# The second layer of an MLP by seven block products, with its weight factors streamed from DRAM and its output turned on VectorE

## The chip, the cores and the metric

The kernel runs on one core of a Trainium2 chip. The metric is device time in microseconds (us). A value is the median of the runs of one kernel; each run of the chip job also ran the kernel before beside it, on the same chip. "Span" is the length of a profiled execution, one to two microseconds shorter than its time.

Names: PE is TensorE's matmul side, PEld its weight loading, DVE VectorE, ACT ScalarE, POOL GpSimd, SP SyncE, which issues nearly all transfers from one in-order queue.

## The reference, cut to what matters

```python
# attention: batch 8, 12 heads, 448 tokens, head_dim 64; q and k RMS-normed, softmax(q k^T / 8) v
x = attn_out.transpose(0, 2, 1, 3).reshape(3584, 768)   # 8 images of 448 tokens
h = x @ w_in             # 768 x 2048
g = h - np.tanh(h)
out = (g @ w_out)        # 2048 x 768, float32
```

The weights arrive as float64 and are rounded to float32 on the chip.

## The kernel before

Image b's MLP runs in the gaps of image b+1's attention; a step is a pair of heads, six steps to an image. A generator yields after every matmul, and each step runs it for four gaps. Image 7's MLP has no attention beside it.

Layer one is already done by seven block products of eight: the matrices are cut in 2x2 blocks, sums and differences of blocks (the factors) are multiplied, and seven products do the work of eight. Image 0 rounds and combines the weight factors, stores them to DRAM, and every image loads them from there through a ring of SBUF tiles (cut):

```python
ring = pool("ring", bufs=8)
ORDER = (1, 6, 5, 2, 7, 3, 4)

def keep_weights():                 # called from weight(), some pieces after set j was combined
    j = kept[1]
    for p in ORDER:                 # seven stores of 384 KB in a row
        nc.sync.dma_start(out=w_in_dram[j, p], in_=built(j, p).rearrange("p f n -> p (f n)"))
    kept[1] = j + 1

def ring_load(to):
    for n in range(len(ring_tiles), min(to, len(ring_steps))):
        b, j, p = ring_steps[n]
        t = ring_tiles[ring_steps[n]] = ring.tile([P, 2, HC, P], F32, name="w_f")
        nc.sync.dma_start(out=t.rearrange("p f c n -> p (f c n)"), in_=w_in_dram[j, p])

def product(j, p, bank, first):     # inside hidden(b), layer one
    k = SETS * 7 * b + 7 * j + ORDER.index(p)
    if b == 0:
        weight(EARLY + k + 1)       # one more weight piece is rounded
    ring_load(k + 7)                # this product and the six after it
    w = ring_tiles[b, j, p]
    for f in range(2):
        for c in range(HC):
            nc.tensor.matmul(bank[:, f * HS : (f + 1) * HS], lhsT=w[:, f, c, :], rhs=moving[p](c), ...)
            ...
```

Layer two is plain. A 128-token tile of g is stationary, half a row of w_out (384 columns, resident in SBUF) moves, and the 64 left-over tokens of two images share a tile, so that images alternate between three and four tiles:

```python
def project(b):
    g = late["g"]
    ring_load(SETS * 7 * (b + 1) + 7)      # the next image's first factors
    units = [(t, n) for t in range(FULL + b % 2) for n in range(2)]
    ...
    for t, n in units:
        for f in range(CF):
            nc.tensor.matmul(ops[:, :HALF], lhsT=lhs[:, f, :], rhs=w_out_sb[f][:, d], ...)
        # ScalarE or VectorE copies the bank to o_sb, SyncE stores it in 1536 B rows
```

## Time and profile before

| | |
|---|---|
| time | 1610.07 us (1609.01 to 1610.49) |
| image 0's MLP beside image 1's attention | 119.6 to 336.7 us of the span |
| images 1 to 6 | 336.7 to 1456.6 us |
| image 7 alone, with the end | 1456.6 to 1608.6 us |
| TensorE / VectorE / GpSimd busy | 96% / 43% / 34% |

The prediction below shows the engine table, the slices and the windows. The first fence is from the page: the DMA row of the 40 slices (tenths of the 16 engines' time) and the queue that carries everything (packets, MB, share of 16 engines).

```profile
DMA  7664974135310452125411244015411144104200
...
q1 hardware_dynamic: 129472, 168.33, 34.6%
```

The row stands at four to nine tenths in slices 1 to 6 and mostly lower after. The second is from the view of the factor loads' source line up to the end of layer one of image 0 (100 to 228 us): who waited for these loads (us, times), and how long they took from issue to landing.

```profile
  POOL w_out L90: 3.8, 2
  PE mc L427: 2.8, 1
...
DMA to landing us min/median/max: 3.7/5.3/8.9
```

TensorE waited for a factor once, 2.8 us, although a load took up to 8.9 us here. Six products of lead, at least 13.6 us at 2.27 us each, covered the rest.

### The profile page before, as it was taken

How to read it: one execution, taken by the hardware profiler on the slowest of the kernel's cores; microseconds unless marked ns; L12 is line 12 of the kernel's file. 1: busy time of each engine (PE TensorE's matmuls, PEld its weight loads, DVE VectorE, ACT ScalarE, POOL GpSimd, SP SyncE). 2: the span in 40 equal slices, each digit the busy share in tenths (PEclk: the TensorE clock that was granted, in tenths of full speed). 3: DMA queues.
4: the chain of work that ended last, by engine and by line, in shares of the span. 5: the costliest groups of instructions: out<-in, count | busy, mean ns of one | idle time of the engine just before them, and what ended most of it. 6: DMA issues, size and time to landing. Idle time of an engine off the chain costs nothing.

```text
span 1608.6 us, 17479 instructions
## 1 busy us (share of the span) xinstructions
PE 1542.8 (96%) x6664; PEld 1018.9 (63%) x6664; DVE 697.1 (43%) x825; ACT 436.4 (27%) x829; POOL 549.8 (34%) x438
## 2 busy tenths in 40 slices
PE   3968799999999999999999999999999999999998
PEld 1327664478655776558855687558755578559954
DVE  6898888543432334234432343333433244221100
ACT  4553354223212232213311133123222123201100
POOL 6655665533422234223322233322432233211200
PEclk9999899999999999999999999999999999999999
DMA  7664974135310452125411244015411144104200
GB/s 197 184 222 148 339 248 125 54 106 154 100 32 28 119 149 91 44 63 153 127 50 32 67 140 148 28 43 151 140 57 32 41 144 145 45 10 142 74 20 22
DMA packets 129889, 169.54 MB, mean 105 GB/s; under 512 B 52485, under 2 KB 93445, under 8 KB 129797
## 3 DMA queue, kind: packets, MB, share of 16 engines
q1 hardware_dynamic: 129472, 168.33, 34.6%
q8 instruction: 55, 0.90, 0.2%
q14 instruction: 38, 0.30, 0.1%
q10 hardware_dynamic: 324, 0.00, 0.0%
HBM read 146.28 MB, written 22.02 MB: 105 GB/s over the span
## 4 chain that ended last, share of the span: by engine, by line
PE 82%; DVE 11%; issue 2%; DMA 2%; POOL 1%; ACT 1%; SPq 0%; ACTq 0%; DVEq 0%; POOLq 0%
PE mb L515 34%; PE mb L427 12%; PE ma L427 8%; PE mc L427 8%; PE sc L327 8%; PE sc L353 7%; DVE w_out L79 3%; PE sc L365 2%; DVE rd L370 2%; DVE w_out L78 1%; POOL sq L280 1%; DVE w_out L82 1%; DVE rr L281 1%; PE sc L303 1%; PE sc L307 1%
## 5 line engine op out<-in xcount | busy, mean ns | idle before, releaser
L515 PE MATMUL mb<-w_out,gT 128*128 128x384 f32 x1536 | 518.2, 492 | 0.0
L515 PEld LDWEIGHTS mb<-w_out,gT 128*128 128x128 f32 x1536 | 287.4, 191 | 221.5 <-issue 37.8
L332 ACT ACTIVATE p<-sc,rr 112x448 f32<-112x448 f32 x384 | 212.6, 636 | 380.4 <-PE sc L327 287.2
L327 PE MATMUL sc<-qT,kT 64*112 64x448 f32 x768 | 179.0, 575 | 5.0 <-DVE rd L370 4.3
L427 PE MATMUL ma<-xT,w_f 128*128 128x224 f32 x768 | 164.7, 362 | 16.9 <-DVE xT L376 11.1
L427 PEld LDWEIGHTS ma<-xT,w_f 128*128 128x128 f32 x768 | 146.4, 194 | 33.0 <-issue 13.7
L427 PE MATMUL mb<-tt,w_f 128*128 128x224 f32 x768 | 156.7, 357 | 5.3 <-DVE u L467 5.3
L370 DVE RECIPROCAL rd<-sc 128x448 f32<-128x448 f32 x42 | 124.0, 2953 | 86.7 <-PE sc L365 86.7
L284 POOL TENSOR_TENSOR rr<-rr,neg_half 112x16 f32<-112x16 f32 x48 | 140.0, 2916 | 50.2 <-DVE rr L283 47.0
L427 PEld LDWEIGHTS mb<-tt,w_f 128*128 128x128 f32 x768 | 144.9, 192 | 16.0 <-issue 8.6
L346 DVE TENSOR_TENSOR sum<-sum,p 112x896 f32<-112x896 f32 x84 | 99.8, 1188 | 111.5 <-ACT p L332 106.2
L280 POOL TENSOR_TENSOR sq<-k_nat 112x512 f32<-112x512 f32 x48 | 53.1, 1106 | 243.8 <-DMA k_nat<-in_k_dram 243.8
L353 PE MATMUL sc<-p,v_nat 112*64 112x448 f32 x672 | 133.4, 539 | 0.0
L327 PEld LDWEIGHTS sc<-qT,kT 64*112 64x112 f32 x768 | 65.1, 177 | 91.3 <-issue 68.7
L281 DVE TENSOR_REDUCE rr<-sq 112x8 f32<-112x512 f32 x96 | 65.6, 684 | 121.9 <-POOL sq L280 121.9
L468 POOL TENSOR_TENSOR u<-u,s 128x448 f32<-128x448 f32 x32 | 38.7, 1208 | 225.0 <-DVE u L467 219.7
L416 POOL TENSOR_TENSOR gT<-s,th 128x448 f32<-128x448 f32 x64 | 74.7, 1170 | 87.8 <-ACT th L414 87.8
L525 DVE COPY o_sb<-mb 128x384 f32<-128x384 f32 x28 | 15.6, 556 | 201.9 <-PE mb L515 201.9
L280 POOL TENSOR_TENSOR sq<-q_nat 112x512 f32<-112x512 f32 x48 | 49.9, 1040 | 142.6 <-DVE rr L281 142.6
L353 PEld LDWEIGHTS sc<-p,v_nat 112*64 112x64 f32 x672 | 48.3, 137 | 78.0 <-issue 76.8
L427 PE MATMUL mb<-xT,w_f 128*128 128x224 f32 x384 | 83.0, 360 | 2.5 <-DVE s L455 2.5
L515 PE MATMUL mb<-w_out,g_rest 128*128 128x384 f32 x256 | 85.4, 489 | 0.0
(79 smaller groups left out, 1493.2 us busy)
## 6 DMA issues: line engine op xcount, KB each, us to landing
w_f<-w_in SPq DMA_DIRECT2D x224, 384.0 KB, 3.3
w_raw<-in_moe_w_out_dram SPq DMA_DIRECT2D x32, 384.0 KB, 3.7
k_nat<-in_k_dram SPq DMA_DIRECT2D x96, 112.0 KB, 3.2
q_nat<-in_q_dram SPq DMA_DIRECT2D x48, 224.0 KB, 3.5
v_nat<-in_v_dram SPq DMA_DIRECT2D x48, 224.0 KB, 4.0
w_in<-w_out SPq DMA_DIRECT2D x28, 384.0 KB, 6.0
out_dram<-o_sb SPq DMA_DIRECT2D x48, 192.0 KB, 1.9
gT<-in_moe_w_in_dram SPq DMA_DIRECT2D x20, 384.0 KB, 5.8
```

Of the source, the lines that this page charges most:

```text
L79: nc.vector.tensor_scalar(out=bits, in0=bits, scalar1=4, scalar2=1, op0=ALU.logical_shift_left, op1=ALU.logical_shift_right)
L280: nc.gpsimd.tensor_tensor(out=sq, in0=rows, in1=rows, op=ALU.mult)
L281: nc.vector.reduce_sum(rr[:, i], sq, axis=AX.X)
L284: nc.gpsimd.tensor_tensor(out=rr2, in0=rr2, in1=neg_half, op=ALU.pow)
L327: nc.tensor.matmul(sc[:CP, :S], lhsT=kT[r, c * CP : (c + 1) * CP], rhs=qT[r, :], start=True, stop=True)
L332: nc.scalar.activation(p[:, h, i, :], tiles[h][:CP, :S], AF.Exp, scale=rr[:, 0, 2 * c + h : 2 * c + h + 1])
L346: nc.vector.tensor_tensor(out=t, in0=t, in1=part, op=ALU.add)
L353: nc.tensor.matmul(av[h * D : (h + 1) * D, :S], lhsT=v_nat[:, h, c, :], rhs=p[:, h, c % 2, :], start=(c == 0), stop=(c == NCH - 1),)
L370: nc.vector.reciprocal(rd, dn[:, :S])
L416: eng.tensor_tensor(out=g[:, f : f + 2, cols], in0=h, in1=th, op=ALU.subtract)
L427: nc.tensor.matmul(bank[:, f * HS : (f + 1) * HS], lhsT=w[:, f, c, :], rhs=moving[p](c), start=(first and f == 0 and c == 0), stop=(f == 1 ...
L515: nc.tensor.matmul(ops[:, :HALF], lhsT=lhs[:, f, :], rhs=w_out_sb[f][:, d], start=(f == 0), stop=(f == CF - 1),)
```

## The change

The intent: layer two also by seven products of eight, on blocks of half the features by half the tokens, in images 1 to 7. The weight factors, now the stationary side, are built once in image 0 and streamed from DRAM like layer one's; g and its combinations move, 224 columns at a time. The output then comes out as features by tokens; VectorE turns it in 32x32 squares, and four transfers per 128 features write rows of 32 floats. Image 0 keeps a plain layer two, turned as well (448 columns moving).

Smaller things go with it. The ring has six slots instead of eight, of larger tiles. The order of products is 1, 5, 6, 2, 7, 3, 4. In image 0 factors are loaded three products ahead instead of six, the sums of attention's steps 6 and 7 go to TensorE, and each half of image 0's MLP gets three steps of attention instead of two and four. A few edits to the first steps and to pools are left out. Cut to its core:

```diff
-    ring = pool("ring", bufs=8)
+    ring = pool("ring", bufs=6)
-    ORDER = (1, 6, 5, 2, 7, 3, 4)
+    ORDER = (1, 5, 6, 2, 7, 3, 4)
+    def combine_w_out(f):                      # image 0, second half of layer two; two ring tiles each
+        t = [ring.tile([P, 8 * P], F32, name="w_f") for _ in range(2)]
+        ...                                    # three VectorE and one GpSimd operation of 128x384
+        for n, count, src in (...):            # four stores in 512 B pieces
+            nc.sync.dma_start(out=w_out_dram[:, n : n + count, :, f, :]..., in_=src...)
+    def ring_load(key, ahead):
+        for n in range(len(ring_tiles), min(ring_steps.index(key) + ahead, len(ring_steps))):
+            ...
+            else:
+                nc.sync.dma_start(out=t, in_=w_out_dram[:, BLOCKS[p], j].rearrange("p f d -> p (f d)"))
     def add(s):
-        if s < NP:
+        if s < NP + 2:                         # sums of steps 6 and 7 go to TensorE
             sums[s] = []
+        def product(j, p, bank, first):        # now shared by both layers
+            if b == 0:
+                weight(EARLY + 7 * j + ORDER.index(p) + 1)
+            ring_load((b, layer, j, p), 4 if b == 0 else 5)
+            ...
+    def store(b, n, y):
+        nc.vector.transpose(out=o, in_=y)
+        for i in range(P // BL):               # four transfers of 128 B rows
+            nc.sync.dma_start(out=out[...].rearrange("(j t) d -> t j d", t=BL), in_=o[...])
     def gap_ns(s):
-        if b == 0:
-            return H_NS / 8 if s % NP < 2 else O_NS * FULL / (4 * (NP - 2))
+        if s < 2 * NP:                         # image 0: three steps for each layer
+            return H_NS / 12 if s % NP < 3 else 4 * S / ENGINE_NS * CD * CF / 12
     ...
```

## The prediction

> **What bounds the kernel now.** I read, in this order: the engine table and the slices of the page, then the windows view (busy time by engine over chosen stretches), the waits of TensorE in the long middle stretch, the chain that ended last, and the groups by shape. The profiled span is 1608.6 us, the timed median 1610.07 us.
>
> Engine table and slices:
>
> ```profile
> PE 1542.8 (96%) x6664; PEld 1018.9 (63%) x6664; DVE 697.1 (43%) x825; ACT 436.4 (27%) x829; POOL 549.8 (34%) x438
> ...
> PE   3968799999999999999999999999999999999998
> ...
> DVE  6898888543432334234432343333433244221100
> ```
>
> One slice is 40.2 us. TensorE is full from the sixth slice on. In slices 1 to 6 VectorE is at eight or nine tenths and TensorE has holes. So there are two regimes, and the border must be found. The windows view does that (columns: window, length, then busy us of each engine, granted clock, DMA share, GB/s):
>
> ```profile
> 119.00:228.00 109.00, 91.95 (x426) 76.85 (x427) 96.81 (x134) 45.75 (x95) 65.28 (x50) 0.90 0.74 245
> 228.00:336.80 108.80, 103.99 (x369) 51.32 (x367) 74.08 (x93) 39.06 (x77) 56.84 (x47) 0.95 0.36 106
> 336.80:1456.00 1119.20, 1119.20 (x4904) 745.23 (x4904) 415.83 (x449) 276.19 (x512) 335.91 (x272) 1.00 0.29 87
> 1456.00:1608.60 152.60, 146.72 (x594) 112.20 (x592) 15.28 (x25) 15.27 (x28) 18.93 (x17) 1.00 0.22 67
> ```
>
> The four stretches are: first layer of image 0, second layer of image 0, images 1 to 6 beside the attention of images 2 to 7, and image 7 alone. In the third, TensorE is busy for all 1119.20 us and VectorE for 37%. The waits view of TensorE's matmul side has no row at all there; its weight-load side waits almost only for "issue", which is load time beside running matmuls and not lost:
>
> ```profile
> PEld sc L353 <- issue: 66.2, 285, 0.2
> ...
> PEld sc L327 <- DVE s L455: 1.2, 6, 0.2
> ```
>
> So from 337 us on the time is TensorE's work and nothing else. The chain and the groups give what that work costs (line 427 is layer one by seven block products, 515 is the plain layer two):
>
> ```profile
> 1504.27 4.54 PE mb L427 x24
> ...
> 1520.16 82.57 PE mb L515 x256
> ```
> ```profile
> L515 PE MATMUL mb<-w_out,gT 128*128 128x384 f32 x1536 | 518.2, 492 | 0.0
> L427 PE MATMUL ma<-xT,w_f 128*128 128x224 f32 x768 | 164.7, 362 | 16.9 <-DVE xT L376 11.1
> ```
>
> Each f32 matmul of the program is two records. The group means of 362 and 492 ns overlap their neighbours; the pitch comes from the chain: 4.54/24 = 0.189 us for 224 columns, 82.57/256 = 0.3225 us for 384. Both are 0.84 ns per column. There is no fixed cost per matmul at either width, so columns can be counted.
>
> **What the Trainium skill says.** "TensorE: Matmul & The Clock Gate", section "Step-by-step: what each phase is for", says that the load of the next stationary tile runs beside the current matmul. The trace agrees at just the width that the new layer two will have: 24 records in 4.54 us, although their weight loads average 192 ns in the group list. "SBUF — State Buffer", section "SBUF: two separate sides", says that a VectorE operation with two SBUF inputs (or in a two-port mode) and a GpSimd operation reading SBUF lock each other out. The early trace agrees: the same VectorE operation of line 79 takes 0.36 us or 1.06 us there. "VectorE: DVE Perf Modes", section "The three transpose paths", gives 311 ns for a 128x128 bf16 turn by 32x32 blocks; no turn on VectorE is in this trace. "DMA: Bandwidth & Descriptors", section "Specifications", puts line rate at 512 B and more, with a read-modify-write below. The new output rows are 128 B; this trace has none of those (its stores are 1536 B rows), so their cost is open.
>
> **The change, part by part.**
>
> *Layer two, TensorE.* Before, image b takes 3 or 4 row tiles, on average 3.5 x 2 halves x 16 = 112 matmuls of 384 columns: 112 x 0.645 = 72.2 us. After, images 1 to 7 take 7 products x 3 sets x 8 = 168 matmuls of 224 columns: 168 x 0.378 = 63.6 us. Image 0 stays plain but turned, 96 matmuls of 448 columns: by 0.84 ns per column 0.752 us each, 72.2 us. So 7 x 8.6 = 60.3 us of TensorE time go. In the stretch from 337 us on this is on the path.
>
> *Vector-side work that comes.* Per image 1 to 7, VectorE gets 8 block subtractions over 448 columns (0.62 us in the like of line 416, so 5 us), 12 evictions of 224 columns (by halves of that, about 0.35 us each, 4.2 us) and 6 turns of 128x448 (estimate 0.55 us from the 0.556 us of the 128x384 copy, 3.3 us), and loses 3 to 4 copies of 0.556 us. Net about +10 us in an image of some 179 us; VectorE goes from 37% to about 44%. GpSimd gets about 10 us more (30% to 37%). Neither bounds. All of it lies beside TensorE.
>
> *Transfers.* Layer two's factors now come from DRAM: 21 loads of 512 KB, 10.5 MiB (11.0 MB) per image, as much as layer one's 28 of 384 KB. Layer one alone on the tail drew about 170 GB/s with no wait, and a load landed in 3.0 to 3.3 us. A load is issued four products ahead, at least 9 us. The rate in layer two is 512 KB per 3.03 us, again 173 GB/s and less beside attention. I expect it hidden.
>
> *Image 0.* Here VectorE sets the pace: 96.81 of 109 us. TensorE's own work in 119 to 337 us is 63.6 + 61.9 (three tiles of 20.6) + 6 attention slots of about 8.5 = 176.5 us; it took 217.2, so some 40 us are lost. The change takes 2 x 3 additions of 1.19 us = 7.1 us from VectorE (the sums of two more steps move to TensorE, which pays 2 x (3.2 - 0.9) = 4.6 us, mostly in holes). I count -6 for VectorE and +1 for TensorE. It adds the building of the factors in the last half of image 0's layer two: 8 groups of 3 additions (about 0.6 us), 15 us of VectorE, and 11 MB written in 512 B pieces within some 50 us, over 200 GB/s. Three of the six ring slots already hold the next image's weights, so the building runs in the other three and can wait for its own writes. I count +4.
>
> *Order of products.* Product 7 accumulates into the bank of product 6, whose eviction must come first. Before, two products lay between (4.5 us); now one (2.27 us in layer one, 3.03 in layer two). When the reciprocal (2.95 us) and the division (0.97 us) come just ahead of that eviction, VectorE can be a microsecond or two late. This can happen once in about five of the 36 slots, so some 4 us in all. End: turn and four short-row stores after the last product instead of a copy, +1.
>
> Sum: 1610.1 - 60.3 - 6 + 1 + 4 + 4 + 1 = 1553.8. I take 1553.
>
> **Rivals.**
>
> *A. TensorE starts to wait for weights in layer two*, because short stores and loads share one in-order issue queue and the same engines. For it: about 10,750 packets of 128 B per image, and a store that waits for its turn on VectorE holds up the loads behind it. Against it: four products of lead, DMA share only 0.29 in the middle. If each product lost 0.5 us, 7 x 21 x 0.5 = 74 us would eat the gain: about 1625. A loss of 0.1 us gives 1568.
>
> *B. VectorE's chain takes over.* The new subtractions wait for GpSimd's output, GpSimd waits for tanh, and VectorE, in order, passes that delay on to the evictions of product 6. For it: GpSimd's power operation is 2.9 us long, and the port lock stretches such pairs. Against it: 37% load, and no wait of TensorE in 1119 us before. At 1.5 us per slot it costs about 55 us: 1608, no gain.
>
> *C. The hand-over at image 0 goes badly:* factor writes back up, image 1's loads queue behind them. The DMA share was already above 0.9 in parts of the first 240 us. It costs once, 10 to 25 us: 1565 to 1580.
>
> *D. Better than expected:* attention is spread over three slots in each half of image 0, so VectorE's and TensorE's loads match there, and half the 40 lost us return: about 1535.
>
> **Range and chances.** The 60 us are counted from a pitch measured at exactly this shape, so they are firm; what varies is the new waits, nearly all upward, with D downward. I predict 1553 us, with 1536 to 1577 as the range. Two per cent is 32 us, a time of 1578. For that half the gain must be lost, which needs A or B in earnest, or C at its worst: faster 0.89, within 2% 0.10, slower 0.01.
>
> **What would show it.** Right: layer two's matmuls of 224 columns at a pitch of 0.189 us in the tail, 63.6 us from the first to the last product of image 7, and a last stage (both layers of image 7) of about 134 us instead of 152.6; images 1 to 6 lasting about 1068 to 1075 us instead of 1119, with TensorE's waits there below 10 us in total and VectorE near 44%; image 1 starting at 335 to 350 us. Wrong: TensorE rows waiting for w_f transfers (A), for evictions of products 6 behind VectorE's subtractions (B), or a hole of over 10 us around 340 us with a DMA share near 1 (C). If a pitch above 0.2 us shows in layer two without a wait, the column count itself fails.

## The result, and the profile after

The changed kernel takes 1590.32 us (1589.75 to 1590.37), the kernel before beside it 1610.28. The ratio is 0.9874, 95% interval 0.9857 to 0.9892. Ratios here are the mean time of one kernel's fast runs over that of the other's of the same rounds, so not quite the ratio of the medians. The change is 20 us faster; 57 were predicted, and the time lies above the predicted range.

From the page of the changed kernel: engines, slices and the DMA queue.

```profile
PE 1494.3 (94%) x7440; PEld 1164.7 (73%) x7440; DVE 788.6 (50%) x1004; ACT 446.4 (28%) x870; POOL 624.4 (39%) x516
...
PE   3988768998999999999999999999999999999997
...
DVE  6788558865454345434544445434544344522211
...
DMA  7554575577545554555554564465454664455564
...
q1 hardware_dynamic: 253552, 256.43, 55.4%
```

TensorE is busy 48.5 us less, as wanted, yet its share has fallen. In slices 5 and 6 VectorE stands at five tenths where it stood at eight, and TensorE at seven and six where it stood at seven and nine. The DMA row now stands at four to seven tenths for the whole span. The windows view, with the same four stages as the prediction cut:

```profile
120.40:263.30 142.90, 108.65 (x493) 83.19 (x493) 99.98 (x137) 52.26 (x108) 70.16 (x54) 0.87 0.61 197
263.30:366.30 103.00, 100.40 (x327) 46.11 (x325) 79.06 (x106) 35.67 (x70) 56.78 (x49) 1.00 0.63 176
366.30:1453.30 1087.00, 1074.29 (x5580) 874.85 (x5579) 488.92 (x589) 282.44 (x546) 395.03 (x333) 1.00 0.53 154
1453.30:1588.60 135.30, 127.08 (x672) 126.73 (x670) 27.00 (x48) 16.48 (x33) 30.77 (x27) 0.99 0.58 165
```

The first stage is the new one: 142.9 us, of which TensorE is busy 108.65 and VectorE 99.98. TensorE is idle for a quarter of it and VectorE for three tenths, at a DMA share of 0.61. The border between the first two stages moved (three steps of attention in each half of image 0 instead of two and four), so image 0 is compared as a whole. "Predicted" is the stage as the prediction's terms make it; its three stages and the 119.6 us of the start add up to a span of 1552.

| stage, us | before | predicted | after |
|---|---|---|---|
| image 0, both layers | 217.1 | 226.4 (+10.3 for 72.2 instead of 61.9 us of layer two, -6 +1 +4) | 245.9 |
| images 1 to 6 | 1119.9 | 1072 (-51.9 of layer two, +4 for the order) | 1087.0 |
| image 7 and the end | 152.0 | 134 | 135.3 |

The 36.6 us between the predicted span and the measured 1588.6 are thus 19.5 in image 0, 15 in images 1 to 6, and about 2 elsewhere.

What TensorE waited for from 90 to 400 us, in the waits view (us in total, times, longest):

```profile
PE mb L448 <- DMA w_f<-w_in: 22.1, 3, 11.0
PE ma L448 <- DMA w_f<-w_in: 11.9, 4, 4.6
...
PE mc L448 <- DMA w_f<-w_in: 2.5, 1, 2.5
```

That is 36.5 us for layer one's own factors, 4.6 of them in image 1 (below). The longest of these waits, in the timeline: the issue queue's rows (start, length, operation, count), then TensorE's row with the wait that ended it, then the window of the hole.

```profile
155.37 6.03 SPq L261 DMA_DIRECT2D w_in<-w_out  x7
161.50 2.11 SPq L296 DMA_DIRECT2D w_f<-w_in  x2
```
```profile
168.04 1.49 PE L448 MATMUL mb<-tt,w_f 128*128 128x224 f32 x3 [10.98 <-DMA w_f<-w_in]
```
```profile
160.00:170.00 10.00, 1.96 (x6) 1.35 (x8) 0.00 (x0) 0.00 (x0) 1.00 (x1) 0.60 1.04 329
```

The seven stores of a factor set, 2.75 MB, take 6.03 us to issue. The load that TensorE needs next stands behind them, is issued at 161.50, and TensorE starts on it at 168.04. In between no compute engine works: VectorE and ScalarE 0.00 of 10 us (GpSimd's 1.00 us ends at 161.04, TensorE's 1.96 us begin at 168.04), DMA share 1.04. The same pattern comes once more, with stores at 207.98 and a wait of 5.81 us that ends at 219.24.

The second place is the hand-over from image 0 to image 1, the same two views:

```profile
371.00 2.64 SPq L275 DMA_DIRECT2D w_out<-w_f  x2
373.74 3.24 SPq L564 DMA_DIRECT2D out_dram<-th  x4
377.02 0.52 SPq L164 DMA_DIRECT2D v_nat<-in_v_dram  x1
377.59 14.09 SPq L296 DMA_DIRECT2D w_f<-w_in  x8
```
```profile
382.05 4.82 PE L448 MATMUL ma<-xT,w_f 128*128 128x224 f32 x12 [4.59 <-DMA w_f<-w_in]
```

The first load of image 1 that is not already in the ring is issued at 377.59, after the last factor writes, the last four short-row stores and the attention loads. Image 1 had begun at 366.3.

From 390 to 1453 us TensorE has one row of waits, where before it had none:

```profile
PE mb L448 <- DVE s L530: 8.1, 6, 1.4
```

It is product 7 of layer one waiting for product 6's eviction. The one wait for a factor in images 1 to 7 is the 4.59 us above. And the tail shows the pitch, in the chain that ended last (start, length, count):

```profile
1514.55 2.27 PE mb L448 x12
1516.82 3.03 PE ma L448 x16
```

3.03/16 is 0.189 us per record, just what layer one has.

### The profile page after: what moved, and what is told of

Same layout as the page of the kernel before. It is cut to its first block, busy times and chain, and to the rows that moved or that the text cites. A ratio compares the mean times of both kernels' runs of the same rounds, so it can differ in the third digit from the quotient of the medians.

```text
span 1588.6 us, 19983 instructions
## 1 busy us (share of the span) xinstructions
PE 1494.3 (94%) x7440; PEld 1164.7 (73%) x7440; DVE 788.6 (50%) x1004; ACT 446.4 (28%) x870; POOL 624.4 (39%) x516
## 4 chain that ended last, share of the span: by engine, by line
PE 74%; DVE 13%; POOL 3%; DMA 3%; issue 2%; ACT 2%; SPq 2%; ACTq 0%; DVEq 0%; POOLq 0%
PE mb L448 24%; PE ma L448 16%; PE mc L448 15%; PE sc L357 8%; PE sc L383 6%; DVE rd L400 2%; DVE w_out L79 2%; PE sc L395 2%; POOL sq L310 2%; DVE sum L376 2%; DMA w_f<-w_in 1%; PE mb L616 1%; DVE rr L311 1%; ACT p L362 1%; DVE w_out L82 1%
## 5 line engine op out<-in xcount | busy, mean ns | idle before, releaser
L448 PE MATMUL mb<-tt,w_f 128*128 128x224 f32 x768 | 166.5, 361 | 17.3 <-DMA w_f<-w_in 16.3
L448 PEld LDWEIGHTS ma<-xT,w_f 128*128 128x128 f32 x768 | 149.7, 197 | 18.7 <-issue 6.2
L315 POOL TENSOR_TENSOR rr<-rr,neg_half 112x16 f32<-112x16 f32 (+1 forms) x49 | 140.7, 2871 | 51.3 <-DVE rr L314 50.3
L448 PE MATMUL ma<-gT,w_f 128*128 128x224 f32 x672 | 139.2, 356 | 0.0
L448 PEld LDWEIGHTS ma<-gT,w_f 128*128 128x128 f32 x672 | 125.3, 190 | 15.3 <-issue 15.3
L448 PE MATMUL mb<-tg,w_f 128*128 128x224 f32 x672 | 135.1, 354 | 0.0
L448 PEld LDWEIGHTS mb<-tg,w_f 128*128 128x128 f32 x672 | 126.2, 190 | 7.3 <-issue 7.3
L376 DVE TENSOR_TENSOR sum<-sum,p 112x896 f32<-112x896 f32 x80 | 95.8, 1198 | 58.2 <-ACT p L362 52.6
L535 POOL TENSOR_TENSOR u<-u,s 128x448 f32<-128x448 f32 x32 | 36.5, 1141 | 221.0 <-DVE u L534 194.7
L448 PE MATMUL mb<-xT,w_f 128*128 128x224 f32 x384 | 87.4, 366 | 17.2 <-DVE s L530 11.4
L448 PEld LDWEIGHTS mb<-xT,w_f 128*128 128x128 f32 x384 | 71.3, 194 | 34.6 <-issue 20.4
```

What stands on the lines that cost most here:

```text
L315: nc.gpsimd.tensor_tensor(out=r, in0=r, in1=neg_half[:, : r.shape[1]], op=ALU.pow)
L376: nc.vector.tensor_tensor(out=t, in0=t, in1=part, op=ALU.add)
L535: nc.gpsimd.tensor_tensor(out=u3, in0=u3, in1=s5, op=ALU.add)
```

## The experiments

Ten kernels ran. Medians below are beside a median of the kernel before of 1610.67, 1611.46 or 1610.89 us in the three chip jobs; the changed kernel's 1590.32 was measured beside 1610.28, so a difference between jobs is known to about 1 us. Stage lengths are read from the timelines of the profiled runs.

### E1: a longer lead in image 0

```diff
-            ring_load((b, layer, j, p), 4 if b == 0 else 5)
+            ring_load((b, layer, j, p), 6 if b == 0 else 5)     # and in image 0 no further into image 1 than before
```

> The changed kernel with one edit: in image 0 the weight factors of layer one are loaded five products ahead instead of three (the ring keeps its six slots; image 1's loads are not moved). Theory (in image 0 a load of w_f stands behind seven stores of w_in in the in-order issue queue, and three products of lead, 7 us, are less than the 6 to 7 us of issue plus 5 to 6.5 us of landing): TensorE's waits for w_f before 262 us, about 32 us with the weight-load side's share, fall below 10 us, layer one of image 0 gets 12 to 22 us shorter, total 1568 to 1578. Rival (VectorE sets image 0's pace anyway, the wait for transfers only takes the place of a wait for VectorE): total within 5 us of 1590, and waits for VectorE grow by as much as those for w_f fall.

Measured: 1576.96 us (1576.12 to 1578.17), ratio to before 0.9791 (0.9775 to 0.9807), so 13.4 us less than the changed kernel. Image 0 takes 232.5 us instead of 245.9; images 1 to 6 take 1086.4, as they did. TensorE's waits from 100 to 262 us:

```profile
PE mb L448 <- DVE s L530: 10.2, 2, 6.1
PE mb L448 <- DMA w_f<-w_in: 9.4, 1, 9.4
PE ma L448 <- DMA w_f<-w_in: 8.6, 2, 4.9
```

The theory holds in the total. The size of the waits was missed: 18.0 us for w_f are left, not under 10, and waits for VectorE came up beside them. So five products of lead are still not always enough, and part of the freed time went into the rival's kind of wait (that VectorE row had 3.3 us in the changed kernel).

### E2: the short lead alone, in the kernel before

```diff
-            ring_load(k + 7)
+            ring_load(k + (4 if b == 0 else 7))
```

> The kernel before with one edit: in image 0 the factors of layer one are loaded three products ahead instead of six; eight ring slots, the old layer two and the old order stay. Theory (short lead is enough by itself): TensorE's waits for w_f in image 0 rise from 2.8 to 20 us or more and the total from 1610 to 1625 to 1635. Rival (the holes of image 0 come from the new layer two, the smaller ring or the spreading over three slots): total within 5 us of 1610.

Measured: 1623.12 us (1621.28 to 1626.44), ratio 1.0078 (1.0061 to 1.0095): 12.5 us slower than before, a little under the range that I gave. Image 0 takes 229.6 us instead of 217.1, which is the whole difference. TensorE's waits over the whole run now hold these rows, where before there was the one of 2.8 us:

```profile
PE ma L427 <- DMA w_f<-w_in: 14.2, 3, 7.8
...
PE mc L427 <- DMA w_f<-w_in: 10.8, 2, 9.2
PE mb L427 <- DMA w_f<-w_in: 2.8, 2, 2.3
```

Without the new layer two, the smaller ring and the new spreading, the lead by itself costs about what E1 wins back.

### E3: the hand-over

```diff
                     combine_w_out(((n - HC) * CF + f) // (HC * CF // HF))
+                    if ((n - HC) * CF + f) // (HC * CF // HF) == HF - 1:
+                        ring_load(ring_steps[7 * SETS], 6)     # image 1's next three factors
```

> The changed kernel with one edit: the next three loads of image 1's layer one factors are issued straight after the last factor group of image 0's layer two is built, ahead of its last factor writes' followers in the issue queue (the k, q, v loads and the last four short-row stores). Theory (at the hand-over the first load missing from the ring is issued only at 377.6 us because 24 us of issue work stand before it in the queue): the wait of 4.6 us at 382 us and the slow products beside it go, total 4 to 10 us lower, 1580 to 1586. Rival (the transfers themselves are saturated there, DMA share 0.95 to 1.0, so issuing earlier only makes them land as late): total within 3 us of 1590.

Measured: 1587.11 us (1585.04 to 1587.59), ratio 0.9852: 3.2 us less, short of the theory's 4 and just past the rival's 3. The wait of 4.6 us at 382 us is gone, no row for w_f is left from 335 to 420 us, and images 1 to 6 take 1079.6 us instead of 1087.0. All of that is in image 1 (181.1 us instead of 188.5). Image 0 took 249.0 us in this profile, 3.1 more, half of it in layer one, before the edit acts; why is not shown. The hole is thus shown to come from issue order. It is worth 7 us in image 1 and about 3 in the total.

### E4: the order of products

```diff
-    ORDER = (1, 5, 6, 2, 7, 3, 4)
+    ORDER = (1, 6, 5, 2, 7, 3, 4)      # and the product loop likewise
```

> The changed kernel with the product order of before (1, 6, 5, 2, 7, 3, 4), so that two products again lie between product 6 and product 7 in one bank. Theory (product 7 waits for product 6's late eviction on VectorE, 8.1 us on TensorE in images 1 to 6): that wait vanishes and the total falls by 5 to 9 us, to 1581 to 1585; image periods fall from about 181 to 179.5 us. Rival (the wait only moves to another bank): period and total unchanged within 2 us.

Measured: 1579.90 us (1577.47 to 1581.28), ratio 0.9805: 10.4 us less. Images 1 to 6 take 1076.8 us instead of 1087.0, and TensorE's waits from 400 to 1440 us are empty, as before the change. The wait did not move to another bank. The middle images take 179.4 us each instead of 181.0, so the gain is a little more than the waits' own 8.1 us.

### E5: the short rows (a wrong result)

```diff
-        for i in range(P // BL):
-            ...                                   # four transfers of 128 B rows
+        rows = out[b * S : (b + 1) * S, :].rearrange("s d -> (s d)")[n * P * S : (n + 1) * P * S]
+        nc.sync.dma_start(out=rows.rearrange("(p x) -> p x", x=S), in_=o)
```

> Wrong on purpose: the changed kernel, but each turned block is written by one transfer of 1792 B rows to consecutive memory instead of four transfers of 128 B rows to their places; everything else is as it was. It measures what the short rows cost. Theory (they lie beside TensorE's work): total within 4 us of 1590, at most the hand-over hole of image 0 gets smaller. Rival (short rows slow the loads of w_f everywhere): total 10 us or more lower, and the landing of w_f<-w_out falls from its median of 4.3 us.

Measured: 1584.36 us (1581.18 to 1585.36), ratio 0.9821: 6 us less, between theory and rival. The landing of the loads did not change; these rows are the two kernels' lists of transfers (count, KB each, median us to landing), the changed kernel first:

```profile
w_f<-w_out SPq DMA_DIRECT2D x147, 512.0 KB, 4.3
...
out_dram<-th SPq DMA_DIRECT2D x192, 56.0 KB, 2.7
```
```profile
w_f<-w_out SPq DMA_DIRECT2D x147, 512.0 KB, 4.3
...
out_dram<-th SPq DMA_DIRECT2D x48, 224.0 KB, 3.1
```

So the rival is out. Two microseconds come at the very end (image 7 and the end take 133.3 us instead of 135.3). The rest lies at the hand-over: images 1 to 6 take 1080.2 us, image 1 alone 182.0 instead of 188.5, and TensorE's wait for w_f after 335 us is 0.8 us. One store instead of four takes less issue time just there (1.18 us instead of 3.24). Image 0 took 2.4 us more in this profile, 248.3. The edit changes two things at once, row length and number of transfers, and no run separates them.

### E6: the three edits together

> The three edits together: lead of five products in image 0, early issue at the hand-over, product order of before. If the three losses are separate, they add: 1590.3 - 13.4 - 3.2 - 10.4 = 1563, between 1559 and 1567. If they overlap (one wait hidden under another) the total stays at 1570 or more. My prediction of 1553 assumed all three to be absent or small; what is left above it then is something else.

E1, E3 and E4 in one kernel. Measured: 1563.43 us (1560.36 to 1564.83), ratio 0.9700 (0.9684 to 0.9716). The three losses add as separate ones do. Image 0 takes 232.2 us and images 1 to 6 1071.5, where the prediction's terms gave 226.4 and, without the 4 us for the order that is undone here, 1068. The waits for w_f before 262 us are 21.4 us.

### E7: stores spread

```diff
-        for p in ORDER:
+        for p in [p for p in ORDER if (j, p) not in stored][: 2 if j > 1 else 7]:
             nc.sync.dma_start(out=w_in_dram[j, p], in_=built(j, p).rearrange("p f n -> p (f n)"))
+            stored.add((j, p))
```

> As the three edits together, and the seven stores of w_in of sets 2 and 3 go two per weight piece instead of seven at once, so that no load of w_f stands behind all seven. Theory (what is left of the waits for w_f in image 0, about 15 us with lead five, comes from that block of stores): waits for w_f before 262 us fall below 6 us and the total is 4 to 10 us below the three edits alone. Rival (a load waits for the landing of its own store, or VectorE sets the pace anyway): within 3 us of it, or slower.

Measured: 1555.71 us (1554.40 to 1557.01), ratio 0.9652 (0.9636 to 0.9668): 7.7 us below E6. The profiled runs are 5.8 us apart: image 0 takes 228.0 us, 4.2 less (layer one 120.2 instead of 129.1, layer two 107.7 instead of 103.0; why layer two grew is not shown), and image 1 takes 2.0 less, where a wait of 1.7 us for w_f is gone. The waits for w_f before 262 us are down to one row, slightly above the 6 us expected:

```profile
PE ma L452 <- DMA w_f<-w_in: 7.0, 2, 4.7
```

This is the fastest version. It gives the right result and beats both kernels, the changed one by 2.2%.

### E8: the sums back on VectorE

```diff
-        if s < NP + 2:
+        if s < NP:
```

> As the three edits together, but the sums of the two steps 6 and 7 go back to VectorE (7.1 us of additions back on VectorE, 4.6 us of matmuls off TensorE). The prediction counted -6 for VectorE and +1 for TensorE, so undoing it should cost 5 us: total 3 to 7 us above the three edits alone. Rival (image 0 is now bound by TensorE and transfers as much as by VectorE): 0 to 5 us faster than the three edits alone.

On top of E6. Measured: 1570.38 us (1566.98 to 1571.87), ratio 0.9743: 7 us slower than E6, at the upper end of what the prediction's -6 and +1 ask for. Image 0 takes 241.6 us instead of 232.2. Moving these sums to TensorE was right.

### E9: stores spread, lead still three

> The changed kernel with only the stores of w_in of sets 2 and 3 spread, two per weight piece instead of seven at once; the lead of image 0 stays at three products, the order and the hand-over as changed. Theory (the two long waits for w_f, 11.0 us up to 168 us and 5.8 us up to 219 us, come from a load standing behind seven stores in the issue queue): both fall below 3 us, total 1574 to 1582. Rival (three products of lead are too few whatever stands in the queue): the waits are spread over more loads, total within 4 us of 1590.

The edit of E7 alone on the changed kernel. Measured: 1580.89 us (1579.92 to 1584.55), ratio 0.9817: 9.4 us less, within the theory's range. The waits from 100 to 265 us say something else, however:

```profile
PE mb L452 <- DMA w_f<-w_in: 14.4, 5, 6.7
PE ma L452 <- DMA w_f<-w_in: 13.8, 3, 6.9
PE mc L452 <- DMA w_f<-w_in: 4.4, 3, 2.1
```

The longest wait fell from 11.0 to 6.9 us, not below 3, and there are eleven waits instead of the changed kernel's seven in this stretch. At the two products behind the blocks of stores the wait fell from 10.98 to 4.88 us and from 5.81 to 1.19; other waits grew, and the sum stayed, 32.6 us against 31.9. So the block of stores makes the two deepest holes, and a lead of three products is too short even without it, as the rival said. Layer one of image 0 did get 9.1 us shorter (133.7 us), but this list does not show where: TensorE's idle time there fell by 5 us, and the time that it counts as busy by 4 (104.58 us instead of 108.65).

### E10: loads ahead of the weight piece

```diff
-            if b == 0:
-                weight(EARLY + 7 * j + ORDER.index(p) + 1)
             ring_load((b, layer, j, p), 6 if b == 0 else 5)
+            if b == 0:
+                weight(EARLY + 7 * j + ORDER.index(p) + 1)
```

> The best version so far (lead five, hand-over, order of before, spread stores: 1555.7) with the loads of w_f issued ahead of the weight piece's own loads and stores within each product. Theory (what is left of layer one of image 0, 120 us against some 108 of before, still has 7 us of waits for w_f): these go, total 1549 to 1554. Rival (VectorE now sets image 0's pace): within 2 us of 1555.7.

On top of E7. Measured: 1558.87 us (1558.69 to 1559.32), ratio 0.9675: 3 us slower, outside both ranges. Image 0 takes 230.4 us. The waits for w_f fall to 4.1 us, but the first of these rows grew from the 0.9 us that it had in E7:

```profile
PE sc L361 <- DVE rd L404: 8.3, 1, 8.3
PE mb L452 <- DVE s L534: 4.1, 1, 4.1
PE ma L452 <- DMA w_f<-w_in: 4.1, 3, 3.0
```

The theory is out. The rows fit the rival, that VectorE now sets image 0's pace: what the loads gave up went to VectorE. But the edit also puts the weight pieces' transfers behind the loads, and no run tells this from VectorE's own work.

## Why the prediction was wrong

**What held.** The terms of the columns held: layer two at 0.189 us per record, 63.7 us from the first to the last product of image 7 for the predicted 63.6, and image 7 with the end 135.3 us for the predicted 134. VectorE's load in images 1 to 6 is 488.92/1087 = 45% for the predicted 44%, GpSimd's 36% for 37%. The factor building costs VectorE 0.60, 0.60 and 0.69 us eight times, 15.1 us for the predicted 15. A turn takes 0.64 us instead of 0.55. No load of layer two's factors made TensorE wait in images 1 to 7.

**The step that failed** is the one under "Transfers": "A load is issued four products ahead, at least 9 us. [...] I expect it hidden." It was written for images 1 to 7, and there it held but for the 4.6 us at the hand-over. But the same line of the diff gives image 0 another number, and there layer one's old loads lost half their lead, from six products to three. The prediction has no term for that, though its own windows showed image 0's first stage at a DMA share of 0.74 before the change, and one more view, the landing of the loads (up to 8.9 us), would have set it against three products of 2.27 us. Image 0 came out 19.5 us above its terms. The trace shows the mechanism, E1 and E2 its size from both sides: 13.4 us won back by two more products of lead, 12.5 us lost in the kernel before by three fewer. E9 and E7 show the second part, seven stores in a block ahead of the load, worth 9.4 us alone and 7.7 us on top of the rest. As they overlap, they don't add in full (13.4 and 9.4 us of image 0 alone, 17.9 together): with both mended, image 0 takes 228.0 us against the 226.4 of the prediction's terms.

The Trainium skill bears on why the block of stores still costs after it is issued: in "DMA: Bandwidth & Descriptors", section "Queues, rings and completion order", it says that descriptors on each DMA engine are consumed in ring order. The trace fits: at a DMA share of 1.04 the load behind 2.75 MB of stores took 6.5 us to land, while the quickest loads of that stage took 3.3.

**A term that was mis-sized: the order of products.** The mechanism was named and is what the waits show (product 7 after product 6's late eviction, up to 1.4 us each). I put 4 us on it; undoing it won 10.4 (E4). My own counts asked for more: one slot in about five of 36, at a microsecond or two, is some 7 to 14 us, not 4. The trace has six waits, 8.1 us in sum.

**Rival C was right in kind, wrong in cause and size.** It expected image 1's loads to queue behind the factor writes, for 10 to 25 us. The hole is there, but a mere change of issue order removes it (E3), for 7 us in image 1 and 3 us net, and the four short-row stores with their 3.24 us of issue time are part of it (E5).

**Rivals A and B as they were put** fell. The short rows left the median landing of layer two's factors at 4.3 us (E5), and in images 1 to 6 VectorE's lateness came only with the order.

**Image 0's other terms.** Moving the sums was worth 7 us (E8) for the -6 and +1 predicted. The +4 for building the factors is not seen on TensorE: in layer two of image 0 VectorE waited 12.4 us for the building's own writes, as feared, but TensorE was busy for 100.40 of the stage's 103.00 us. Of rival D, half of the 40 lost us returning, little is seen: even in E7 image 0 takes 228.0 us for 191 us of TensorE's work (63.6 + 72.2 + 51 of attention + 4.6 of sums), so about 37 are still lost.

That E7 ends within 3 us of the predicted 1553 is partly luck: it has the old order, so that the terms without the 4 us for the order, a span of 1548, are its measure. Its span is 1552.7, about 1.5 us more in each of image 0, images 1 to 6 and the end. What stays open is how much of image 0's rest VectorE's own chain holds; E10 only hints at it.

## What to carry to other kernels

When a change takes buffers from a ring, ask of every stage that shares the ring how many transfers ahead it now is, and set that against the landing times of that stage, not of the quiet one. A load is as early as its place in the in-order issue queue allows: a block of stores in front of it cost 6.03 us of issue here, and the load then took 6.5 us to land, so spread such stores or give the loads more lead. And when two products share an accumulator, look at how late the first one's eviction can be: here, beside attention, one product between them left six waits of up to 1.4 us, and two left none.

## What the Trainium skill lacked or had wrong

- "DMA: Bandwidth & Descriptors": the section "Anatomy of one DMA — SWDGE (gpsimd) path" gives about 50 ns for the sequencer's dispatch, and no page gives a time for what a transfer from SyncE costs its queue while the engines are busy. Here, from 100 to 265 us, a 384 KB load took 0.33 to 1.06 us of the queue (median 0.43), and the seven stores in a row 6.03/7 = 0.86 us each.
- "DMA: Bandwidth & Descriptors", "Specifications": it names the read-modify-write below 512 B but no cost of such stores for a neighbour. Here four transfers of 128 B rows instead of one of 1792 B rows left the landing of the loads beside them at 4.3 us, and cost about 6 us in all, 2 of them at the end of the kernel.
- "VectorE: DVE Perf Modes", "The three transpose paths": the time is for 128x128 bf16 alone (311 ns), and no page has one for float32. A 128x448 float32 turn from SBUF to SBUF took 0.63 to 0.64 us.
